# Retention and a mixer on one core: casting row loads, decay moved to mask and v, crossbar turns, a turned token mixing and zero products

## The chip, the core and the metric

The program runs on one core of a Trainium2 chip. The metric is the device time of one execution in microseconds (us), taken for several executions. The kernel before took 228.76 us in the median of three runs (227.15 to 229.37).

The engines are TensorE (PE: matrix products; its weight loads are shown apart as PEld), VectorE (DVE), ScalarE (ACT), GpSimd (POOL) and SyncE (SP, which here only issues DMA transfers). Each runs its own instructions in order, and they wait for one another by semaphores.

## The reference, cut to what matters

Batch 4, 8 heads, 768 tokens, 64 columns a head. Everything comes and goes as f32.

```python
gamma = 1.0 - 2.0 ** (-5.0 - arange(H))            # one decay per head
for t in range(S):                                 # retention
    state = gamma * state + outer(k[t], v[t])
    y[t] = q[t] @ state / sqrt(D)
x = y, heads side by side                          # B x 768 x 512
u = x + (relu(x.T @ w_tok1) @ w_tok2).T            # token mixing, 768 -> 256 -> 768
out = u + relu(u @ w_ch1) @ w_ch2                  # channel mixing, 512 -> 1536 -> 512
```

Both kernels cut the tokens into six chunks of 128 and take two heads (a "pair") at a time: four pairs a batch, 16 in all. Inside a chunk the recurrence is a masked product of scores (k q, then mask, then times v), and between chunks a state is carried. The decay is put in by factors per token and head, called `gk` (on the k side) and `gy` (on the y side). The work on one pair up to the mixed rows u is called "front" and the two channel products of a batch "back".

## The kernel before

Rows come as f32 from the sync queue. DVE scales k by `gk` and casts it, and POOL casts q and v:

```python
        for nm, src in (("k", k), ("q", q), ("v", v)):
            ...
                    dma = nc.sync.dma_start(out=t, in_=rows.rearrange("h (c p) d -> p (h c) d", p=P))
            ...
        kc = op("DVE", 900, 980, emit, [ld["k"]], [K], [sl["k"]])
        ...
        qc = op("POOL", 770, 830, cast(Q, sl["q"]), [ld["q"]], [Q], [sl["q"]])
        vc = op("POOL", 770, 830, cast(V, sl["v"]), [ld["v"]], [V], [sl["v"]])
```

k, q and later u are turned on PE, as six products with the identity, and copied out by ACT or DVE:

```python
                for c in range(NC):
                    nc.tensor.transpose(tp[:, c * P:(c + 1) * P],
                                        src.tile[:, c].rearrange("p h d -> p (h d)"), ident16)
```

The order of the instructions is decided by a small scheduler inside the kernel. It keeps a clock for each engine, gives each step an estimated cost, and lists the steps. That listing is each engine's order. The lines that matter later are these:

```python
                start = free[op.eng]
                for d in op.deps:
                    if d.eng == op.eng and (d.dma or d.eng == "PE"):
                        continue                      # this dependency costs no time
                    start = max(start, d.end + (30 if d.eng == op.eng else SEM) + op.guard)
```

A dependency on a step of the *same* engine is passed over if that step is a DMA or a PE step. For the scheduler a DMA's engine is the one that *issues* it. In this kernel the rows are issued by SP, which computes nothing, so the line never hides a load from the step that consumes it.

## Time and profile before

| | before |
|---|---|
| time | 228.76 us (227.15 to 229.37, 3 runs) |
| first channel product of batch 0 | 42.1 us |
| last front part ends | 154.3 us |
| PE busy from 42.1 to 224.3 us | 177.9 of 182.3 us |
| POOL busy | 68.6 us |

From the page of the kernel before come the totals, PE and POOL in 40 slices of 5.7 us (a digit is the busy share in tenths), the make-up of the chain of waits that ended last (a name with q is that engine's sequencer, which also issues DMAs; "issue" is time in which the profile shows nothing waited for), and one group of instructions (busy us, mean ns of one, then the idle time before them and who ended it):

```profile
span 228.0 us, 4873 instructions
...
PE 204.1 (90%) x1968; PEld 131.4 (58%) x1968; DVE 114.9 (50%) x287; ACT 115.9 (51%) x219; POOL 68.6 (30%) x120
...
PE   0467797799999999959999999999999999999993
...
POOL 2429935831045347243355424130000000000000
...
PE 77%; ACT 6%; DVE 5%; issue 3%; POOL 3%; SPq 3%; DMA 2%; DVEq 0%; POOLq 0%; ACTq 0%
...
L237 POOL CAST v<-vf 128x768 f16<-128x768 f32 x16 | 13.6, 851 | 8.8 <-PE fa L335 4.9
```

PE is full from the ninth slice on and makes up 77% of the chain. POOL has room. The v casts stood idle for 8.8 us in all over 16 pairs; only 3.8 us of that was for rows of v, and the q casts waited another 8.3 us for rows of q. So POOL stood still for rows for some 12 of 228 us.

### The profile page before, as it was taken

The page shows a single profiled execution, that of the slowest core. Times are in us where ns is not written, and L with a number is a line of the kernel's source. Part 1 is how long each engine was busy: PE and PEld are TensorE (multiplying, and loading weights), DVE is VectorE, ACT ScalarE, POOL GpSimd, SP SyncE. Part 2 cuts the span into 40 slices and gives each one's busy share as a digit, 9 for nine tenths or more (in the row PEclk, how much of TensorE's full clock was granted, in tenths as well). Part 3 has the DMA queues.
Part 4 walks back from the last instruction along what each step waited for, and adds up shares of the span by engine and source line. Part 5 has one row for each costly group of instructions (what it writes and reads, how often), then busy time and mean ns, then how long its engine had stood idle before and what let it go on. Part 6 is the DMA issues. An engine that isn't in the chain of part 4 may idle for free.

```text
span 228.0 us, 4873 instructions
## 1 busy us (share of the span) xinstructions
PE 204.1 (90%) x1968; PEld 131.4 (58%) x1968; DVE 114.9 (50%) x287; ACT 115.9 (51%) x219; POOL 68.6 (30%) x120
## 2 busy tenths in 40 slices
PE   0467797799999999959999999999999999999993
PEld 0255596455576676746777757674554554645541
DVE  6388944101879888885799887621202103012021
ACT  2255346473599864557877741762360540721700
POOL 2429935831045347243355424130000000000000
PEclk9999999799999999988999999999999999999999
DMA  7999999999999999991000011101201202103012
GB/s 181 241 241 223 206 208 204 242 243 228 259 290 244 264 235 223 275 277 24 0 3 3 0 49 46 52 0 49 92 0 50 88 3 92 46 5 127 9 46 92
DMA packets 65814, 29.41 MB, mean 129 GB/s; under 512 B 50432, under 2 KB 62720, under 8 KB 65792
## 3 DMA queue, kind: packets, MB, share of 16 engines
q1 hardware_dynamic: 61568, 25.17, 47.6%
q0 software_dynamic: 4224, 3.93, 10.6%
q8 instruction: 15, 0.25, 0.5%
q14 instruction: 7, 0.06, 0.1%
HBM read 26.74 MB, written 6.29 MB: 145 GB/s over the span
## 4 chain that ended last, share of the span: by engine, by line
PE 77%; ACT 6%; DVE 5%; issue 3%; POOL 3%; SPq 3%; DMA 2%; DVEq 0%; POOLq 0%; ACTq 0%
PE ba L459 27%; PE ba L483 27%; PE tp L250 4%; PE fa L378 4%; ACT qT L259 4%; PE fa L311 3%; PE tp L420 3%; PE fa L396 3%; DMA vf<-in_v_dram 2%; PE fa L335 2%; DVE am L318 2%; PE ba L378 2%; PE fa L332 2%; SPq L213 1%; SPq L209 1%
## 5 line engine op out<-in xcount | busy, mean ns | idle before, releaser
L459 PE MATMUL ba<-uT,wc 128*128 128x384 f16 x384 | 71.8, 334 | 0.0
L472 ACT ACTIVATE h<-ba 128x384 f16<-128x384 f32 x96 | 47.0, 493 | 46.1 <-PE ba L459 45.7
L483 PE MATMUL ba<-wc,h 128*128 128x512 f16 x288 | 67.8, 379 | 0.0
L491 DVE TENSOR_TENSOR o<-x,ba 128x512 f32<-128x512 f32 x24 | 16.5, 686 | 74.7 <-PE ba L483 74.7
L459 PEld LDWEIGHTS <-wc 128*128 128x128 f16 x384 | 36.5, 100 | 23.1 <-issue 2.5
L483 PEld LDWEIGHTS <-h 128*128 128x128 f16 x288 | 26.5, 98 | 27.5
L318 DVE TENSOR_TENSOR am<-fa,mask 128x384 f16<-128x384 f32 x64 | 33.1, 549 | 9.4 <-PE fa L311 9.2
L259 ACT COPY qT<-tp 128x768 f16<-128x768 f16 x16 | 23.2, 1449 | 13.7 <-PE tp L250 13.1
L367 POOL CAST x<-x 128x384 f16<-128x384 f32 x32 | 16.6, 521 | 37.7 <-ACT x L348 34.4
L410 POOL CAST u<-x 128x384 f16<-128x384 f32 x32 | 15.9, 510 | 24.5 <-DVE x L403 24.2
L284 DVE SCALAR_TENSOR_TENSOR U<-U,gp,fa 128x64 f32<-128x64 f32 x64 | 17.5, 275 | 1.2
L348 ACT ACTIVATE x<-fa,gy 128x192 f32<-128x192 f32 x40 | 14.4, 420 | 6.7 <-PE fa L335 6.7
L230 DVE TENSOR_SCALAR k<-kf,gk 128x384 f16<-128x384 f32 x32 | 15.9, 537 | 3.4 <-DMA kf<-in_k_dram 3.3
L237 POOL CAST q<-qf 128x768 f16<-128x768 f32 x16 | 13.7, 858 | 12.0 <-DMA qf<-in_q_dram 8.3
L429 ACT COPY uT<-tp 128x768 f16<-128x768 f16 (+1 forms) x20 | 13.4, 672 | 7.6 <-PE tp L420 7.5
L403 DVE TENSOR_TENSOR x<-x,fa 128x384 f32<-128x384 f32 x24 | 12.5, 551 | 8.6 <-PE fa L396 7.4
L335 PE MATMUL fa<-v,am 128*128 128x64 f16 x192 | 15.9, 204 | 0.6 <-DVE am L318 0.6
L237 POOL CAST v<-vf 128x768 f16<-128x768 f32 x16 | 13.6, 851 | 8.8 <-PE fa L335 4.9
L335 PEld LDWEIGHTS <-am 128*128 128x128 f16 x192 | 13.9, 105 | 3.4 <-DVE am L318 1.0
L250 PE MATMUL tp<-ident,k 128*128 128x128 f16 x96 | 9.6, 248 | 6.8 <-DVE k L230 5.2
L378 PEld LDWEIGHTS <-wt 128*128 128x128 f16 x192 | 13.4, 107 | 3.0 <-issue 1.4
L311 PE MATMUL fa<-qT,kT 64*128 64x128 f16 x192 | 12.0, 237 | 2.8 <-ACT qT L259 2.7
(46 smaller groups left out, 184.2 us busy)
## 6 DMA issues: line engine op xcount, KB each, us to landing
kf<-in_k_dram SPq DMA_DIRECT2D x16, 384.0 KB, 6.5
qf<-in_q_dram SPq DMA_DIRECT2D x16, 384.0 KB, 6.0
vf<-in_v_dram SPq DMA_DIRECT2D x16, 384.0 KB, 5.7
out_dram<-o SPq DMA_DIRECT2D x24, 256.0 KB, 2.0
wc<-in_moe_w_ch_dram POOLq DMA_DIRECT2D x6, 512.0 KB, 9.9
wt<-in_moe_w_tok_dram POOLq DMA_DIRECT2D x2, 384.0 KB, 6.6
```

Source lines behind the costliest of these rows:

```text
L237: nc.gpsimd.tensor_copy(t.rearrange("p c h d -> p h c d"), src.tile.rearrange("p (h c) d -> p h c d", h=2))
L250: nc.tensor.transpose(tp[:, c * P:(c + 1) * P], src.tile[:, c].rearrange("p h d -> p (h d)"), ident16)
L259: (nc.scalar.copy if eng == "ACT" else nc.vector.tensor_copy)(d, o)
L284: nc.vector.scalar_tensor_tensor(U[:, c], U[:, c - 1], gp[:, p:p + 1], o, ALU.mult, ALU.add)
L311: nc.tensor.matmul(a[j][:, i], KT.tile[r, t], QT.tile[r, t], start=True, stop=True)
L318: nc.vector.tensor_tensor(am, src[:, :HC], mask, ALU.mult)
L335: nc.tensor.matmul(o[:, j * D:(j + 1) * D], AM[2 * hf + j].tile[:, i], V.tile[:, c, j], start=(c == 0), stop=(c == 0 or j == 1))
L367: nc.gpsimd.tensor_copy(X16.tile[:, half(hf)], X.tile[:, half(hf), pc])
L378: nc.tensor.matmul(acc[:, jt * P:(jt + 1) * P], wt1[:, i, jt * P:(jt + 1) * P], X16.tile[:, i], start=(i == 0), stop=(i == NC - 1))
L459: nc.tensor.matmul(acc[:, :SH], w[:, ct, (ft % FW) * P:(ft % FW + 1) * P], UT.tile[:, ct, sh * SH:(sh + 1) * SH], start=(ct == 0), stop=(c ...
L472: nc.scalar.activation(H2.tile[:, ft], A.tile[:, :SH], AF.Relu)
L483: nc.tensor.matmul(A.tile, H2.tile[:, ft, i * P:(i + 1) * P], wc2[ft // FW][:, ft % FW], start=(ft == 0), stop=(ft == NF - 1))
```

## The change

The intent is to take work from PE, which is the bound: k, q and u are turned by the DMA engines' crossbar instead, from batch 1 on. The turns take the f16 rows as they land, so the loads become casting DMAs, which are issued by POOL. k can then not be scaled before it is turned, so `gk` goes into a mask per head and into a scaled copy `vs` of v that only the state products use. In batch 0 the second token mixing is also computed in turned form, so the first channel product no longer waits for add, cast, turn and copy. Zero products fill early gaps of PE. The scheduler may now choose between engines for some steps (`either`).

```diff
-                dma = nc.sync.dma_start(out=t, in_=rows.rearrange("h (c p) d -> p (h c) d", p=P))
+                        nc.gpsimd.dma_start(out=t[:, :, i],          # k and q: one head each, casting
+                                            in_=src[b, 2 * p + i].rearrange("(c p) d -> p c d", p=P))
+                        nc.gpsimd.dma_start(out=t, in_=src[b, 2 * p:2 * p + 2].rearrange(
+                            "h (c p) d -> p (h c) d", p=P))          # v: both heads
 ... (rows of f32, k scaling and q, v casts removed; six buffers each for k, q, v)
         def turn(src, dst, dep):
+            if not first:
+                    nc.sync.dma_start_transpose(out=t.rearrange("d (c t) -> d c t", t=P),
+                                                in_=flat(src.tile))
+                return Op((0, b, p, 0), [("SP", 100, 100, emit)], [dep], [dst], [src], dma=800)
+        vs = op(either(emit, DVE=(500, 560), POOL=(1100, 1200)),
+                [vl, g_op], [VS], [V])
 ... (mask times gk per head; batch 0's second mixing also turned; u turned by crossbar)
+                for w in op.ways:
+                    start = max(base, free[w[0]])
+                    for d in op.deps:
+                        if d.eng == w[0] and (d.dma or d.eng == "PE"):
+                            continue
+                        start = max(start, d.end + (30 if d.eng == w[0] else SEM) + op.guard)
+    FILL, F_ON, F_NS = 0.7, 30000, 165
+                    nc.tensor.matmul(spare[:, :384], zero[:, :P], zero, start=True, stop=True)
```

(Comments are added here; cuts are marked by "...".)

## The prediction

> **What bounds the kernel now.** I read first the busy time by stretch, then the chain that ended last, then the groups, then the queues of the stage in which TensorE (PE) is not full. The stretches, cut where the first channel product of batch 0 starts (42.1 us) and where the last front part ends (154.3 us):
>
> ```profile
> 0.00:42.10 42.10, 26.20 (x325) 21.46 (x326) 26.81 (x83) 18.89 (x38) 23.01 (x44) 1.00 1.19 215
> 42.10:154.30 112.20, 107.85 (x1274) 73.74 (x1272) 77.76 (x189) 72.47 (x132) 45.64 (x77) 0.97 0.66 146
> 154.30:224.40 70.10, 70.01 (x372) 36.17 (x370) 9.68 (x15) 24.57 (x50) 0.00 (x0) 1.00 0.14 53
> ```
>
> The columns are window, length, busy time of PE, PE weight loads, VectorE (DVE), ScalarE (ACT) and GpSimd (POOL), PE clock, DMA share, GB/s. Up to 42 us PE is busy for 26 of 42 us and the DMA engines are full (share 1.19, overlapping packets). From 42 us on PE is busy 177.9 of 182.3 us: it is the bound, and every PE instruction removed there counts. The chain gives the unit costs (start, us, what):
>
> ```profile
> 18.03 0.82 PE tp L250 x6
> ...
> 42.12 9.48 PE ba L459 x48
> ...
> 54.62 0.34 PE tp L250 x6
> ...
> 58.26 0.27 PE fa L311 x6
> ...
> 92.44 0.67 PE fa L378 x12
> ...
> 193.17 7.80 PE ba L459 x48
> 200.97 7.77 PE ba L483 x36
> ```
>
> A turn of six blocks is 0.34 us on PE when warm, 0.82 us at 18 us; 48 first channel products (L459) are 7.80 us at the end but 9.48 us at 42 us. So PE is slow early. The other queues of the first stage:
>
> ```profile
> 2.59 2.13 SPq L213 DMA_DIRECT2D kf<-in_k_dram  x1
> ...
> 7.35 1.97 SPq L213 DMA_DIRECT2D kf<-in_k_dram  x1
> ...
> 12.08 2.24 SPq L213 DMA_DIRECT2D kf<-in_k_dram  x1
> ...
> 39.30 0.37 SPq L213 DMA_DIRECT2D kf<-in_k_dram  x1
> ```
> ```profile
> 18.37 1.77 POOL L172 DMA_DIRECT2D wt<-in_moe_w_tok_dram  x2
> 24.35 3.71 POOL L172 DMA_DIRECT2D wc<-in_moe_w_ch_dram  x5
> 46.91 0.83 POOL L237 CAST v<-vf 128x768 f16<-128x768 f32 x1 [0.98 <-DMA vf<-in_v_dram]
> ```
>
> The k issues, 4.75 us apart, are the pace at which a full DMA takes one pair of heads. Rows of batch 1 start at 39.3 us, behind the weights, and the first pair is complete at 46.9 us (its v cast starts). A casting issue costs POOL 0.74 to 0.9 us.
>
> **What the Trainium skill says.** "TensorE: Matmul & The Clock Gate", part 1 (the HAM clock gate): PE starts at half rate and needs about 3.4 us of sustained work to reach the full one; idle falls back. The trace agrees: 0.82 against 0.34 us above (0.82 holds an end of about 0.2 us), and 9.48 - 7.80 = 1.68 us is what 3.4 us at half rate costs. "DMA: Bandwidth & Descriptors", section SWDGE vs HWDGE vs iDMA: only GpSimd can issue a casting DMA, so the loads move from the sync queue to POOL; here all eight casting weight loads are indeed POOL's. Same page, Latency and other measured facts: DMA transposes ran at 261 GB/s in one kernel. Estimate from it: 128x768 f16 is 0.197 MB, so 0.75 us each; no run here shows it yet. "SBUF — State Buffer", door 1 (the "DVE blocks DMA" trap): descriptors made by GpSimd starve while DVE runs a two-port operation; I can't see it in this trace, so it widens the range upwards.
>
> **The change part by part.**
>
> *PE, after batch 0.* k and q of batches 1 to 3 and their mixed rows u are turned by crossbar DMA: three turns per pair, 12 pairs, 36 x 0.34 = 12.2 us less on PE. One pair in front is now state products 0.28, scores 2 x 0.28, y 2 x 0.34 (in the timeline a chunk of three products takes 0.115 us), token mixing 0.67 + 2 x 0.34: 2.87 us instead of 3.89. The channel part is unchanged: 8 x (7.80 + 7.77) = 124.6 us. So the work from the first channel product falls from 12 x 3.89 + 124.6 = 171.3 to 12 x 2.87 + 124.6 = 159.0 us. Before, 171.3 us of work took 182.2 us (42.1 to 224.3): 10.9 us over, of which 112.20 - 107.85 = 4.35 idle, 1.7 cold, 4.9 left for the changes between products that PE makes at each group.
>
> *First stage.* The second token mixing of batch 0 is computed already turned, x is added through the identity, so the chain add, cast, turn, copy (0.55 + 0.51 + 0.34 + 0.48 us for each half, serially visible at 39 to 42 us) is replaced by one copy; PE does both forms, eight more groups of about 0.34 to 0.5 us, but PE has 16 us to spare there. The order of the changed kernel puts all of it before the first channel product. q copies lose their odd pattern (1.45 to 0.80 us on ACT). The decay goes to a mask per head and to v: 32 k scalings of 0.54 us (15.9 us) leave DVE, v scalings come, mostly on POOL. All this lets the first channel product start about 8 us earlier: v of the last pair lands about 24 us, then some 13 steps with about 9.5 us of work and semaphores, so 34 us. The zero products keep PE warm: another 1.7 us.
>
> *But the gain of the start is capped by DMA.* Bytes read are the same and the packets, still one per row of 256 bytes, nearly so; rows of batch 0 (4 x 4.75 = 19 us), eight weights (some 19.5 us), then batch 1. In the changed order PE does 48 L459 products and two of the next group, 8.2 us, and then the state products of batch 1's first pair, in order. These need that pair's v (about 48 us, as 46.9 now) and its scaling on POOL (2 x 0.52 us): about 49.5 us. PE will reach that point at 34 + 8.2 = 42 and wait some 7 us. Now the same point is passed at 52.0. So of about 10 us only about 2.5 arrive.
>
> *Sum.* 49.5 + (159.0 - 8.2) + tail 3.7 (228.0 - 224.3) = 204.0 us, plus overheads. Changes between groups shrink with the number of groups, 8 instead of 11 to 12 a pair: about 3.5 us. Idle from late data: 2 to 5 us. That is 210.
>
> *Other engines in the middle.* From 49.5 us to the pure channel stretch at the end (order: the last 46 + 3 x 48 L459 and 4 x 36 L483, about 62 us) PE has 150.8 - 62 = 88.8 us, 7.4 us a pair. DMA: loads 4.75 + three transposes 2.25 + one output of some 0.7 = 7.7 us a pair. POOL: four half loads of k and q at 0.8, v 0.9, v scaling 1.04, casts of x and u 4 x 0.51: 7.2 us a pair. DVE and ACT lie lower: ACT loses 12 x (0.80 + 1.45 + 0.80) = 37 us of copies. So three things run at nearly the same pace; loads have up to two pairs of lead (six buffers instead of two to four), but waits of this kind are likely.
>
> **Rivals.** (a) POOL binds: if a half load of 768 rows costs 1.06 us (the first weight load, also 768 rows, took that of the 1.77 us above) and v 1.6 us, a pair costs POOL 8.9 us: 12 x 1.5 = 18 us more, 222 to 226. Against it: loads with 256 and 512 rows took 0.72 and 0.77, which gives 0.81 for 768. (b) DMA binds: if each crossbar turn costs 1.6 us of all engines, a pair takes 10.3 us, 12 x 2.9 = 35 us against 5 us of lead: about 230. The 261 GB/s speak against it; nothing in the trace tests it. (c) Casting halves the bytes written and speeds the loads to 3 x 1.5 us a pair: batch 1 arrives at 46 us, middle waits vanish: 202 to 204. (d) The latency of a crossbar turn is on no path: k and q have a product group of 4.8 us between the state products and the scores, u is wanted a batch later. So no loss there.
>
> **Range and chances.** 210 us, 201 to 221. Below 201 both caps would have to vanish; above 221 rival (a) or (b) has to be real at half strength. Removing 12.2 us of PE work from a PE-bound stretch is the firmest term and alone gives 5%; slower needs (b). Faster by over 2% 0.93, within 2% 0.05, slower 0.02.
>
> **What will show it.** First L574 product (the channel product of after) near 34 us, first L362 of batch 1 near 49 us with an idle PE before it; v rows landing as the releaser. PE busy in the middle over 93%. Pure stretch at the end 62 us long, tail 3.7 us. POOL busy about 114 us (64 halves x 0.8, 16 x 0.9, 6.2 weights, 26 scalings and 46 casts at about 0.52, 5 for the rest). The 48 first channel products at 7.8, not 9.5 us. I am wrong if PE waits on POOL's v scaling or on crossbar turns for over 10 us in the middle, or if the rows of batch 1 land well after 50 us.

## The result, and the profile after

| | before | after |
|---|---|---|
| median of the runs beside each other, us | 229.06 (227.15 to 229.5, 4 runs) | 295.28 (294.67 to 297.07, 4 runs) |
| ratio after to before | | 1.2918 (95%: 1.2849 to 1.2987) |

All four runs of after agree within 1%, and e4 below took as long. Executions over 1.5% slower than the fastest of the same kernel are left out of the means. The results were correct. Here and below a ratio is the mean time of one kernel's fast runs over that of the other's of the same rounds, so it isn't quite the ratio of the medians quoted beside it.

The change costs 29%; the prediction was 8% faster. This is the page of after, in the same parts as above:

```profile
span 294.1 us, 4616 instructions
...
PE 222.6 (76%) x1827; PEld 135.9 (46%) x1827; DVE 100.2 (34%) x259; ACT 94.4 (32%) x212; POOL 132.8 (45%) x176
...
PE   8819989655594939633939294929699999999994
...
POOL 8969530948558393819291929190522100000000
...
PE 35%; POOL 30%; DMA 28%; issue 4%; DVE 1%; POOLq 0%; ACT 0%; ACTq 0%
...
L350 POOL TENSOR_SCALAR vs<-v,gk 128x384 f16<-128x384 f16 x26 | 32.0, 1235 | 75.8 <-DMA v<-in_v_dram 58.7
```

Read the two slice rows together, one under the other. In slices 19 to 28 (7.35 us each) POOL goes 9, 2, 9, 1, 9, 2, 9, 1, 9, 0 and PE goes 3, 9, 3, 9, 2, 9, 4, 9, 2, 9: one is full where the other stands, with a period of two slices, 14.7 us. Two rows that swing against each other with the period of one unit of work suggest engines that wait for each other in turn, and no engine that is the bound by its amount of work. POOL is busy for only 45% and yet holds 30% of the chain. The last line says what it does in between: it stood 75.8 us in front of the scaling of v, 58.7 us of that until a DMA of v landed.

What PE waited for is in the list of its waits (engine and line, what it waited for, us in all, times, longest):

```profile
PE bank L471 <- POOL x L460: 49.1, 16, 8.8
PE bank L362 <- POOL vs L350: 14.7, 6, 5.6
```

L471 is the first token mixing, which needs POOL's cast of x, and L362 are the state products, which need POOL's scaling. The casts stand in POOL's queue behind the scaling, so they come late with it.

The windows of after have the columns of the prediction's windows (window, length, busy PE, PEld, DVE, ACT, POOL, PE clock, DMA share, GB/s). They are cut where the first state products of batch 1 start and where the pure channel stretch begins:

```profile
0.00:54.60 54.60, 42.05 (x452) 28.68 (x453) 26.67 (x90) 25.75 (x55) 35.78 (x50) 0.93 1.35 134
54.60:228.30 173.70, 118.58 (x1045) 74.78 (x1045) 64.58 (x156) 45.14 (x109) 96.08 (x125) 0.78 0.96 92
228.30:290.40 62.10, 61.91 (x334) 32.44 (x332) 8.45 (x14) 23.52 (x48) 0.97 (x2) 1.00 0.15 55
```

The loss is all in the second row: 173.70 us for 12 pairs, 14.5 us a pair, against the 88.8 us (7.4 us a pair) of the prediction. PE is idle for 55.1 us of it. Its granted clock is only 0.78 there, against 0.97 in the middle of before, so its work is longer too; this agrees with the page of the Trainium skill that the prediction cites, "TensorE: Matmul & The Clock Gate", part 1, by which an idle PE falls back to the lower rate.

What a pair's 14.5 us consist of can be read from POOL's timeline in the middle of after (start, length, instruction, and in brackets the idle time before it with what ended it):

```profile
175.33 2.46 POOL L350 TENSOR_SCALAR vs<-v,gk 128x384 f16<-128x384 f16 x2 [5.85 <-PE bank L430]
...
182.42 1.02 POOL L287 DMA_DIRECT2D v<-in_v_dram  x1
189.99 2.46 POOL L350 TENSOR_SCALAR vs<-v,gk 128x384 f16<-128x384 f16 x2 [6.55 <-DMA v<-in_v_dram]
192.41 1.70 POOL L283 DMA_DIRECT2D k<-in_k_dram  x2
```

POOL issues the v load of a pair at 182.42 us. Its very next instruction is the scaling of *that same v*, so POOL stands for 6.55 us until the rows have landed, scales for 2.46 us, and only then issues the k load of the next pair. One lap, from 175.33 to 189.99 us, is 2.42 us of scaling, 5.69 us for five issues with three casts between them, and 6.55 us of standing: 14.66 us. (The wait in front of 175.33 us is put down to PE's L430. The scaling does not use what L430 makes; these products ended just before the scaling started, 6.9 us after the issue of its v, so we read this wait too as one for v. Three waits are of this kind, 17.0 of the 75.8 us.) There are six buffers for each of k, q and v, but the loads never run ahead, because the engine that would issue them waits for the previous ones.

The chain of waits of after shows the same lap, and an end that is as predicted (start, length, what):

```profile
182.42 7.38 DMA v<-in_v_dram
...
197.53 7.83 DMA v<-in_v_dram
...
228.26 7.48 PE bank L574 x46
...
282.44 7.78 PE bank L601 x36
290.25 0.69 DVE o L609
```

The two v loads are 15.1 us apart, and each is on the chain. The channel stretch from 228.26 to 290.25 us is 62.0 us long.

### The profile page after: what moved, and what is told of

Same layout as the page of the kernel before. It is cut to its first block, busy times and chain, and to the rows that moved or that the text cites. A ratio compares the mean times of both kernels' runs of the same rounds, so it can differ in the third digit from the quotient of the medians.

```text
span 294.1 us, 4616 instructions
## 1 busy us (share of the span) xinstructions
PE 222.6 (76%) x1827; PEld 135.9 (46%) x1827; DVE 100.2 (34%) x259; ACT 94.4 (32%) x212; POOL 132.8 (45%) x176
## 3 DMA queue, kind: packets, MB, share of 16 engines
q0 software_dynamic: 79232, 13.37, 61.7%
## 4 chain that ended last, share of the span: by engine, by line
PE 35%; POOL 30%; DMA 28%; issue 4%; DVE 1%; POOLq 0%; ACT 0%; ACTq 0%
DMA v<-in_v_dram 24%; PE bank L601 14%; PE bank L574 14%; POOL k L283 8%; POOL vs L350 7%; POOL q L283 7%; DMA wc<-in_moe_w_ch_dram 5%; POOL x L460 3%; POOL u L538 3%; PE bank L522 2%; PE bank L471 2%; POOL gyw L633 1%; PE bank L405 1%; POOL v L287 1%; PE bank L430 1%
## 5 line engine op out<-in xcount | busy, mean ns | idle before, releaser
L601 PE MATMUL bank<-wc,h 128*128 128x512 f16 x288 | 74.1, 407 | 0.0
L574 PE MATMUL bank<-uT,wc 128*128 128x384 f16 x384 | 72.1, 341 | 0.0
L350 POOL TENSOR_SCALAR vs<-v,gk 128x384 f16<-128x384 f16 x26 | 32.0, 1235 | 75.8 <-DMA v<-in_v_dram 58.7
L588 ACT ACTIVATE h<-bank 128x384 f16<-128x384 f32 x96 | 46.8, 489 | 57.4 <-PE bank L574 57.1
L471 PE MATMUL bank<-x,wt 128*128 128x128 f16 x192 | 19.0, 258 | 49.2 <-POOL x L460 49.1
L413 DVE TENSOR_TENSOR am<-bank,mask 128x384 f16<-128x384 f32 x64 | 32.6, 548 | 52.9 <-PE bank L405 52.6
L601 PEld LDWEIGHTS <-h 128*128 128x128 f16 x288 | 27.6, 102 | 31.7 <-issue 5.8
L471 PEld LDWEIGHTS <-wt 128*128 128x128 f16 x192 | 15.6, 116 | 54.1 <-issue 52.5
L443 ACT ACTIVATE X<-bank,gy 128x192 f32<-128x192 f32 x56 | 20.0, 418 | 39.7 <-PE bank L430 39.5
L283 POOL DMA_DIRECT2D k<-in_k_dram x32 | 27.3, 857 | 0.7 <-DMA wt<-in_moe_w_tok_dram 0.7
L283 POOL DMA_DIRECT2D q<-in_q_dram x32 | 26.6, 837 | 2.3 <-DVE uT L503 2.1
L362 PE MATMUL bank<-vs,k 128*64 128x64 f16 x160 | 7.6, 229 | 14.9 <-POOL vs L350 14.7
L522 PEld LDWEIGHTS <-wt 128*128 128x128 f16 x192 | 16.8, 126 | 3.5 <-issue 2.5
L430 PEld LDWEIGHTS <-am 128*128 128x128 f16 x192 | 14.8, 109 | 4.8 <-issue 2.8
```

Source lines behind the costliest of these rows:

```text
L283: nc.gpsimd.dma_start(out=t[:, :, i], in_=src[b, 2 * p + i].rearrange("(c p) d -> p c d", p=P))
L350: (nc.vector if e == "DVE" else nc.gpsimd).tensor_scalar(t[:, :, j], V.tile[:, :, j], gk[:, h:h + 1], None, ALU.mult)
L413: nc.vector.tensor_tensor(am, src, m, ALU.mult)
L430: nc.tensor.matmul(o[:, j * D:(j + 1) * D], AM[2 * hf + j].tile[:, i], V.tile[:, c, j], start=(c == 0), stop=(c == 0 or j == 1))
L443: nc.scalar.mul(X.tile[:, half(hf), h * D:(h + 1) * D], yv[:, :, j * D:(j + 1) * D], gy[:, h:h + 1])
L471: nc.tensor.matmul(acc[:, jt * P:(jt + 1) * P], wt1[:, i, jt * P:(jt + 1) * P], X16.tile[:, i], start=(i == 0), stop=(i == NC - 1))
```

## The experiments

The theory after the first reading (theory 1) was: the lap "issue v, wait for it, scale it, issue the next pair" on POOL's in-order queue costs the time. Rivals were that casting loads are slow in themselves or beside the turns (2), and that the crossbar turns hold the loads up (3). Each ran on one chip beside runs of the kernel before, so times are compared with those (e9 to e12 had the same chip): medians of 229.33 us for e1 to e4, 229.27 for e5 to e8, 229.31 for e9 to e11, 229.30 for e12, and 228.80 for e13 and e14. All kernels but e3 gave correct results. Where an edit refers to "e1" and so on, it stands on top of that kernel; e1 to e4 and e13 stand on after.

### e1_vs_dve: the scaling on DVE only

```diff
-        vs = op(either(emit, DVE=(500, 560), POOL=(1100, 1200)),
+        vs = op(either(emit, DVE=(500, 560)),
```

> The changed kernel, with the v scaling allowed on DVE only, so that nothing on POOL waits for a load that POOL itself has just issued. Theory 1 (POOL stalls in order behind its own v load, some 6 us a pair, and so issues the next loads late): the pair rhythm of 14.5 us falls to 7 to 9 us, time 210 to 230 us, POOL waits for v near 0. Theory 2 (the DMA engines are full: casting rows of 128 bytes written plus crossbar turns take some 14 us a pair whatever the order): time stays at 280 us or more and the waits for v move to DVE or to the issues.

Measured: 226.07 and 228.09 us in the fast runs, one slow at 229.49, and the profiled run slow at 328.93 us with a granted clock of 0.564. The ratio is 0.9933 (0.9806 to 1.0059): the same as before. Nearly the whole loss of 66 us goes with one entry in a list of allowed engines. So the loads and turns themselves, all still there, do not cost it. The edit does two things at once, it takes the scaling's time from POOL and the wait out of POOL's queue; e2 separates them. And it is not 210 us either: measured against the prediction, a second loss of some 16 us lay hidden behind the first.

### e2_loads_ahead: the scaling stays on POOL, the next pair's loads go in front of it

```diff
+    for op_ in [o for o in order if o.eng == "POOL" and o in scalings]:   # batches 1 to 3
+        at = order.index(op_)
+        nxt = [o for o in order[at:] if o in row_loads][:5]
+        for o in nxt:
+            order.remove(o)
+        at = order.index(op_)
+        order[at:at] = nxt
```

> The changed kernel; the only edit: in batches 1 to 3 the five load issues of the next pair stand ahead of a pair's v scaling on POOL, PE's order is the same. Theory 1: a pair costs POOL 4.4 us of issues + 2.46 of scaling + about 2 of casts = 8.9 us instead of 14.5, so 11 x 5.6 = 60 us less, 228 to 245 us. Theory 2: 280 us or more, the wait moves to the issues.

Measured: 237.84 us (236.97 to 240.71, the last a slow run), ratio 1.0445 (1.0331 to 1.056). Here every scaling that was POOL's still is, at the same cost. Only the order of POOL's queue is different, and 57 us of the 66 are gone. The wait for v fell from 58.7 us to this (engine and line, what it waited for, us in all, times, longest):

```profile
POOL vs L352 <- DMA v<-in_v_dram: 7.1, 4, 3.2
```

One lap of its POOL timeline is now

```profile
85.26 2.51 POOL L352 TENSOR_SCALAR vs<-v,gk 128x384 f16<-128x384 f16 x2
...
92.36 1.05 POOL L288 DMA_DIRECT2D v<-in_v_dram  x1
93.41 2.51 POOL L352 TENSOR_SCALAR vs<-v,gk 128x384 f16<-128x384 f16 x2
```

that is 8.15 us without a gap. The scaling is again right behind an issue of v, but of a later v. POOL is now nearly full: it is busy for 90.16 of the 102.00 us from 54 to 156 us. This kernel is some 11 us slower than e1, where the scaling is DVE's. From the first to the last state products of batches 1 to 3 a pair takes 9.24 us here and 8.65 in e8 (e1 without the zero products, below), which makes 6.5 us, and they start at 53.9 and not at 49.2 us, which makes 4.7. (The edit leaves the order of batch 0 as it was in after.)

### e3_rates: loads and turns by themselves

This kernel computes nothing (its output is zeros). It loads eight pairs by casting, eight as f32 from the sync queue, makes twelve turns alone, and then eight casting pairs beside 24 turns, each part behind the one before.

```diff
+    for p in range(8): cast_pair(p // 4, p % 4)          # then wait for the last
+    for p in range(8): full_pair(p // 4, p % 4)          # f32, sync queue; then wait
+    for i in range(12): turn(g)                          # then wait
+    for p in range(8):
+        cast_pair(2 + p // 4, p % 4)
+        for i in range(3): turn(g)
```

> No computation, the result is wrong on purpose (zeros). Four stages, each waiting for the one before: 8 pairs of heads loaded by casting DMA as in the changed kernel; 8 pairs as f32 from the sync queue; 12 crossbar turns alone; 8 pairs by casting DMA with 24 crossbar turns beside them. Theory 1 needs a casting pair in 7 us or less, also beside turns in 9 us or less. Theory 2 needs 10 us or more for a pair alone, or 13 us or more beside turns. f32: 4.8 to 5.3 us. A turn alone: 0.75 us by the 261 GB/s, 1.4 us by the packets' time in the trace of after.

Measured, one look at 179.38 us (its state is unknown): small DVE copies mark the landings. Two v loads in the casting part, then the last three turns of the part with turns alone (start of the copy, and in brackets how long DVE waited for the landing):

```profile
34.79 0.16 DVE L86 COPY g<-v 128x1 f16<-128x1 f16 x1 [1.87 <-DMA v<-in_v_dram]
...
39.20 0.16 DVE L86 COPY g<-v 128x1 f16<-128x1 f16 x1 [2.24 <-DMA v<-in_v_dram]
...
92.49 0.16 DVE L86 COPY g<-turned 128x1 f16<-128x1 f16 x1 [1.20 <-DMA turned<-g]
...
95.15 0.16 DVE L86 COPY g<-turned 128x1 f16<-128x1 f16 x1 [1.19 <-DMA turned<-g]
```

The last two casting pairs land 39.20 - 34.79 = 4.4 us apart, and so do the last two f32 pairs from the sync queue (73.29 and 77.70 us). From the first issue to the last landing eight pairs took 38.0 us by casting and 38.3 as f32, 4.7 and 4.8 us each. Casting is neither slow nor fast; theory 2 falls. The turns land (95.15 - 92.49) / 2 = 1.33 us apart, where the prediction had 0.75. Beside each other, eight casting pairs, each with three turns, took 62.5 us, 7.8 us a pair, far from the 13 us or more that theory 2 needed there. But with the output, which the prediction put at 0.7 us a pair, this is more than the 7.4 us that PE needs, so a second loss can come from here.

### e4_pe_turns: k and q turned on PE in every batch

```diff
         def turn(src, dst, dep):
-            if not first:
+            if False:
```

> The changed kernel with the turns of k and q back on PE in all batches (u stays with the crossbar): 24 of 36 crossbar turns gone, 8.2 us more PE work. Theory 1: the rhythm of POOL stays, 280 to 300 us. Theory 3 (the crossbar turns hold up the loads): v lands 2 to 4 us sooner, time 240 to 265 us.

Measured: 295.57 us (293.89 to 295.81), ratio 1.2913 (1.2809 to 1.3016), the same as after. Two thirds of the crossbar turns are gone, PE does them, and nothing changes: POOL waits 56.6 us for v as before. As the cause of the first loss, theory 3 falls. The run also shows that PE can take on 24 turns for nothing while something else holds it up.

### e5_vs_dve_again: e1 once more, for a fast profile

> The same kernel as e1_vs_dve (v scaling on DVE), because the profiled run of that one fell into a half PE clock (0.56) for its whole length. Time 226 to 230 us again. If the DMA engines bind its middle (a casting pair 4.4 us, three turns of 1.33 us, an output of about 0.8 us, 9.2 us a pair one after the other, 8.6 as they overlapped in e3_rates), the first state products of successive pairs lie 8 to 9 us apart, and PE waits for turned k or q and for v. If PE bound it as predicted, they lie 7.4 us apart and PE has hardly any waits.

The kernel is that of e1. Measured: three runs at 225.28 to 227.18 us, ratio 0.9898 (0.9802 to 0.9994). The time of e1 is confirmed, but the profiled run was a slow one again, this time of 685.1 us, so no fast profile came of it. One line of its chain of waits is worth a look:

```profile
649.52 29.63 PE bank L601 x36
```

The same 36 products take 7.78 us in after.

### e6_dve_pe_turns and e7_dve_pe_q: fewer crossbar turns

On top of e1, e6 turns k and q on PE, and e7 q alone:

```diff
-            if not first:
+            if False:                           # e6
+            if not first and dst is KT:         # e7: only k goes by crossbar
```

> e1_vs_dve with the turns of k and q back on PE in all batches. If the DMA engines bind e1, this frees 2.7 us of DMA a pair for 0.68 us of PE: DMA 6.5, PE 8.1 us a pair, 212 to 222 us. If the crossbar is not what binds e1, PE's 8.2 us more make it 230 to 238 us.

> e1_vs_dve with only the turns of q back on PE in all batches: DMA 7.9, PE 7.75 us a pair. If the DMA engines bind e1: between e1 and e6, 214 to 224 us. Otherwise 230 to 234 us.

Measured: e6 215.94 us (215.10 to 217.97), ratio 0.9452 (0.9366 to 0.9538); e7 217.63 us (217.35 to 219.16), ratio 0.9531 (0.9439 to 0.9623). Both are as expected. Giving 24 turns *back* to PE, some 24 x 0.34 = 8 us more of its work, makes the kernel about 11 us faster than e1. With the first loss gone, the crossbar turns cost more than they save. Whether by the DMA's time or by the order in which PE waits for them, e12 tells.

### e8_dve_nofill: e1 without the zero products

```diff
-    FILL, F_ON, F_NS = 0.7, 30000, 165
+    FILL, F_ON, F_NS = 0.0, 30000, 165
```

> e1_vs_dve without the zero products. If they only warm PE before a stage in which the loads set the pace, 226 to 230 us, the same as e1. If the cold PE sets the start, 231 to 236 us.

Measured: 226.00 us (223.78 to 226.54), ratio 0.9860 (0.9771 to 0.9949), which is unclear against before and overlaps e5's runs of 225.28 to 227.18 us. The zero products are worth nothing here. Its profile, a fast one, serves as that of e1. The largest item of PE's waits, then PE's timeline from the first channel products to the first state products of batch 1, then the middle as a window:

```profile
PE bank L405 <- DMA qT<-q: 14.4, 9, 3.8
```
```profile
37.03 7.96 PE L574 MATMUL bank<-uT,wc 128*128 128x384 f16 x48
44.83 4.48 PE L601 MATMUL bank<-wc,h 128*128 128x512 f16 x20
49.24 0.35 PE L362 MATMUL bank<-vs,k 128*64 128x64 f16 x10
```
```profile
37.00:155.00 118.00, 102.24 (x1087) 64.64 (x1085) 72.83 (x185) 50.00 (x121) 68.15 (x100) 0.94 1.68 151
```

The first state products of batch 1 run at 49.24 us (the prediction: 49.5) and the last ones at 144.4 us, so a pair takes 95.2 / 11 = 8.65 us, not 7.4. PE stands 14.4 us in front of the scores for a turned q.

The pace follows the number of crossbar turns. From the first to the last state products of batches 1 to 3 a pair takes 8.65 us here with three turns, 7.1 in e7 with two (49.5 to 127.7 us) and 6.2 in e6 with one (49.1 to 117.1 us), though PE has 0.34 us more to do at each step.

### e9_e6_nofill, e10_e6_price, e11_e7_price: the scheduler is told the right price

The scheduler estimates a turn at 800 ns. e9 is e6 with FILL 0.0; e10 is e9, and e11 is e7 without zero products, both with the measured price:

```diff
-    FILL, F_ON, F_NS = 0.7, 30000, 165
+    FILL, F_ON, F_NS = 0.0, 30000, 165                # e9, e10, e11
-                return Op((0, b, p, 0), [("SP", 100, 100, emit)], [dep], [dst], [src], dma=800)
+                return Op((0, b, p, 0), [("SP", 100, 100, emit)], [dep], [dst], [src], dma=1330)
-                   [UT] if opens else [], [U16] if opens else [U16, UT], dma=800)
+                   [UT] if opens else [], [U16] if opens else [U16, UT], dma=1330)     # e10, e11
```

> e6_dve_pe_turns without the zero products. If they only warm PE for a stage that the loads pace, 213 to 217 us, the same as e6 or a little less, as in e8 against e1. If they are worth their place: 218 to 221 us.

> e9, and the kernel's own scheduler told that a crossbar turn takes 1330 ns of DMA, as measured in e3_rates, instead of 800; only u is turned there by now. If the order of instructions costs anything through the wrong price: 208 to 213 us. If not, the same as e9 within 1 per cent.

> e7_dve_pe_q without the zero products and with the same price of 1330 ns; k and u turned by the crossbar. If DMA work of 7.9 us a pair binds it, the order can't help: 214 to 218 us. If the waits came from a wrong order: 208 to 213 us.

Measured: e9 216.11 us, ratio 0.9423 (0.9394 to 0.9451); e10 215.12 us, ratio 0.9389 (0.9366 to 0.9411); e11 **211.61 us** (211.15 to 213.91), ratio 0.9250 (0.9184 to 0.9315). e9 shows again that the zero products are worth nothing. The price does little for e10, whose only turns are those of u, wanted a batch later. e11 is 6 us faster than e7 (0.925 against 0.953). Its edit has two parts, but the zero products were worth nothing in e8 and e9, so we put the gain down to the price: in e11 a turned k is wanted soon. Its middle is

```profile
42.00:140.00 98.00, 93.80 (x1106) 61.49 (x1105) 71.46 (x182) 51.37 (x115) 68.98 (x104) 1.00 1.83 145
```

with PE busy for 93.80 of 98 us at full clock. This version beats both kernels.

### e12_e8_price: all turns on the crossbar, with the right price

e8 with both `dma=800` made `dma=1330`.

> e8_dve_nofill (all three turns by the crossbar, v scaling on DVE, no zero products) with the scheduler's price of a turn at 1330 ns. If the DMA engines bind the middle (8.6 us a pair), the order can't help: 221 to 226 us, the same as e8's 226.0 within 2 per cent, and the state products of successive pairs stay 8.4 to 8.8 us apart. If the wrong price and so the order made the waits for turned q: 209 to 216 us and 7.4 to 7.9 us a pair.

Measured: 218.16 us, ratio 0.9508 (0.9479 to 0.9536). This is between the two expectations, so neither was right as it stood. The pace of the front stayed where the DMA puts it, 8.57 us a pair (state products from 50.4 to 144.7 us), against 8.65 in e8. But PE's wait for the turned q fell from 14.4 us to this:

```profile
PE bank L405 <- DMA qT<-q: 0.5, 1, 0.5
```

With the late turn known, the scheduler puts channel products of the batch before in front of the scores: after the state products at 74.81 us ten products of L601 follow, where e8 has two after those at 76.47 us and then waits 1.77 us for q. The same late data then cost less, because PE has other work at that moment. A pace set by DMA is a loss only as far as PE has nothing else to do.

### e13_sees_load: only the scheduler's condition is mended

The remaining question was why the listing puts the scaling right behind its own load. The condition shown in the kernel before answers it: now the load is *issued* by POOL, so for the way "scaling on POOL" its landing is passed over. The scheduler believes that v is there at once. For the way "scaling on DVE" it does count the landing, so POOL looks better, though it was entered at twice the cost. The test changes that line and nothing else. POOL remains allowed, and prices and turns are those of after:

```diff
-                        if d.eng == w[0] and (d.dma or d.eng == "PE"):
+                        if d.eng == w[0] and d.eng == "PE":
```

> The changed kernel with one condition of its own scheduler corrected: an operation on the engine that issued a DMA now counts as waiting for that DMA to land (until now POOL's scaling counted as free to start right after POOL had issued the load). Nothing else is edited; the scheduler then puts all but two pairs' scalings on DVE and the other two behind the loads of the next pair. If this condition is the cause of the order that costs the time: 224 to 232 us, as e1. If something else in the change costs it: 260 us or more.

Measured: 221.38 and 222.42 us in fast runs, 227.46 and 227.00 in slow ones, beside 228.80 of before. The fast runs are 1.6 and 2.6 us better than the expected range, the slow ones lie in it. The scheduler now chooses DVE for all but two pairs' scalings, and those two stand on POOL behind later loads; this is one of them, with no idle time in front:

```profile
70.79 2.49 POOL L350 TENSOR_SCALAR vs<-v,gk 128x384 f16<-128x384 f16 x2
```

So the loss of 66 us goes with one condition. It is the root of the first loss. Two of its four runs took about as long as e1; why the other two are some 5 us shorter was not tested.

### e14_all_fixed: e11 with the mended condition in place of the ban on POOL

```diff
-        vs = op(either(emit, DVE=(500, 560)),
+        vs = op(either(emit, DVE=(500, 560), POOL=(1100, 1200)),
-                        if d.eng == w[0] and (d.dma or d.eng == "PE"):
+                        if d.eng == w[0] and d.eng == "PE":
```

> e11 (turns of q on PE, no zero products, a crossbar turn priced at 1330 ns) with that condition corrected in place of the ban of POOL from the scaling: one pair's scaling goes to POOL, behind a later load. 210 to 214 us, the same as e11's 211.6 within 1 per cent, if the ban did nothing but hide the wrong condition.

Measured: 214.26 us (213.82 to 215.40), ratio 0.9385 (0.9335 to 0.9436). That is 1.3% more than e11, on another chip, and slightly outside what was expected. Part of it may be the order that the choice of engines brings; that was not taken further. The best version stays e11.

## Why the prediction was wrong

The direction was wrong: 210 us was predicted with 0.93 for faster, and 295.28 us came. Step by step:

**The start came near in number once the first loss is removed, but not in the way that was said.** The cap by the rows of batch 1 was put at 49.5 us, with an idle PE in front of it. In e8 the first state products run at 49.24 us, but PE does not idle: from 44.83 us it runs 20 of the second channel products, where the order that the prediction read had two. So that agreement is in part luck. The first channel product was put at 34 us and came at 37.0 us in e8. In after itself it came at 42.88 us, no earlier than the 42.1 us of before: the first loss acts in batch 0 already. (It came at 42.78 us in e2, which leaves batch 0 alone, and at 36.44 in e13.) POOL waits 2.32 us for v of one of its pairs, scales it from 19.66 to 22.13 us, and only then issues the last two loads of that batch. And v of batch 1's first pair is scaled from 52.07 us, and the last of its state products start at 54.58 us.

**The end was right.** The pure stretch is 62.0 us (62 predicted), and from 290.25 us to the end of the span at 294.1 us are 3.8 us (3.7).

**The step that failed is in "Other engines in the middle": "loads have up to two pairs of lead (six buffers instead of two to four), but waits of this kind are likely".** The lead does not exist. A buffer lets a load start early only if its issuer gets to issue it. POOL's 7.2 us a pair was treated as an amount of work, to be compared with PE's 7.4, and rival (a) too asked only how long an issue takes. (The issues came near the sum: 0.85 us in the mean for a half load of k or q and 1.03 for v, where 0.8 and 0.9 were put.) But POOL's queue is in order, and each pair's v load stands in it right in front of an instruction that needs that load. So the wait for a load came into every pair's lap, 3.5 to 7.2 us in the eleven laps of the middle. Of POOL's 173.7 us in the middle, some 63 us are this standing: 75.8 us in front of all the scalings, less 2.3 and 10.4 us in front of two early ones. It could have been seen before the run: the changed kernel's order on POOL lists v load, scaling of the same v, next k load, pair after pair, and the order was at hand, for the prediction quotes parts of it. The prediction even named the sign, "I am wrong if PE waits on POOL's v scaling", and gave it no weight; PE waited 14.7 us for the scaling and 49.1 us for POOL's casts behind it. e2 shows that the order alone makes 57 of the 66 us, and e13 shows where the order comes from.

**A size of the same step was off too.** The scaling on POOL was put at 2 x 0.52 = 1.04 us a pair, from the casts. It measured 2 x 1.235 = 2.47 us. That makes up POOL's busy time, 132.8 us where 114 was predicted: 26 x (1.235 - 0.52) = 18.6 us, about the whole difference.

**The second loss is rival (b), at part strength.** Three turns a pair were 2.25 us in the sum of the DMA. They are 3 x 1.33 = 4.0 us. The pace of a pair is then not 7.7 us but about 8.6 (8.65 in e8, 8.57 in e12), and with the first loss cured the kernel takes 226 us and not 210. Twelve pairs at 8.65 - 7.4 = 1.25 us would be 15 us of those 16, if PE found nothing else to do. e6 confirms it from the other side, since fewer turns are faster though PE has more to do. e12 limits it: at the same pace 8 us come back when the order counts with the late turn, so about half of the second loss is the DMA's pace with PE standing in front of it because of the order. What the rest is made of was not taken apart further. The 261 GB/s of "DMA: Bandwidth & Descriptors" was the wrong base for this size of turn. (The rival's own sum is also off: 35 less 5 us on top of the 204.0 us are 234, not 230.)

**Rival (d), that the latency of a turn is on no path, was wrong for q** in the order of e8: 14.4 us of PE's waits there are for it. In e12's order it is 0.5 us. **Rival (c), faster loads by casting, did not come**: 4.7 us a pair by casting against 4.8 in e3. The packets did not stay nearly the same either: POOL's queue has 79232 in after, where before it had 4224 and the sync queue, outputs included, 61568. No loss of time from it is seen, since a casting pair of e3 takes no longer than the 4.75 us of before. The risk that DVE starves POOL's descriptors shows nowhere in the issues: a half load of k or q holds POOL for 0.82 to 0.87 us in the lap of after from 175.33 us, and for 0.82 us in the last part of e3, where DVE does nothing.

**The zero products were worth nothing** (e8 against e5, e9 against e6), where the prediction had 1.7 us. There was nothing left to warm up: the 48 first channel products took 7.96 us in after, and 7.96 us in e8 and e9 without any zero products, where before had 9.48. The granted clock is 1.00 there in e8 (37 to 46 us) and was 0.83 in before (42 to 52 us). Which part of the change made them quicker was not tested.

e11 comes near the prediction's 210 us, but it is another kernel: its scaling is off POOL, the turn has its measured price, q is turned on PE and there are no zero products. That the numbers agree does not bear out the sum.

## What to carry to other kernels

When a load moves to an engine that also computes, read that engine's queue as an order and not as a sum: an instruction that needs a load, standing right behind the issue of that load, puts the whole latency into every lap, however many buffers there are. A scheduler's shortcut such as "same engine, so no wait" must be checked again when the issuer of a DMA changes. Measure the price of the new form of an operation by itself, here 1.33 us for a turn, before it is weighed against the one it replaces, and give that price to whatever makes the order.

## What the Trainium skill lacked or had wrong

- "DMA: Bandwidth & Descriptors", Latency and other measured facts, gives 261 GB/s for transposes in one kernel. Here a turn of 128x768 f16 (0.197 MB), twelve in a row with nothing else, took 1.33 us, which is 148 GB/s.
- The same page, Anatomy of one DMA, calls descriptor generation a small part of the fixed cost. It does not say how long an issue keeps POOL from its next instruction, and that is not small: a casting issue of one head's rows held POOL for 0.82 to 0.87 us, one of two heads' rows for 1.02 us. (The page's about 1 us to the first byte on this path is of the same size.) At five a pair that is 4.4 us of POOL's time; e3's issues alone ran at 4.25 us a pair.
- "GPSIMD Engine Reference", section 4.1 Engine selection, says that one-input elementwise work on GpSimd is roughly at line rate. Here scaling 128x384 f16 by a value per partition took 1.235 us on POOL, and a median of 0.394 us on DVE (e8). A cast of 128x384 f32 to f16 took 0.52 us on POOL, so the number of inputs alone does not tell; whether the instruction or the types make the difference was not tested.
- "TensorE: Matmul & The Clock Gate", HAM trace caveats, warns that the clock's records may be unreliable. In the slow run of 328.93 us the record says 0.564, but in that of 685.1 us it says 1.0, while 36 products took 29.63 us instead of 7.78.
